# GpSimd's weight sums placed one pass earlier behind row transfers, and ScalarE's copy of a pair placed ahead of the previous pair's activations

## The chip, the cores and the metric

The kernel runs on one core of a Trainium2 chip. Its time is device microseconds for one execution; the times given are medians over several executions. The engines are TensorE (PE; PEld is its weight load), VectorE (DVE), ScalarE (ACT), GpSimd (POOL) and SyncE (SP, which here issues most of the DMAs). Each engine takes its instructions in program order and waits on semaphores for the others.

## The reference

Two stages, all in float32. The first is a linear attention with a decaying state over 4 batches, 8 heads, 768 steps and a head dimension of 48. The second routes each of the 3072 resulting rows of 384 values to one of 8 experts:

```
logits = x @ w_gate                       # 3072 x 8
expert_idx = argmax(logits)               # one expert a token
gate_w = softmax(logits)[expert_idx]
for e in range(8):
    xe = x[expert_idx == e]
    h  = relu(xe @ w1[e])                 # 384 -> 1024
    ye = h @ w2[e]                        # 1024 -> 384
    out[expert_idx == e] = gate_w * ye
```

## The kernel before, in words

The attention takes the first 150 us or so. Tokens are sorted on the way by an indirect DMA into an area of `rows` in HBM for each expert. The experts then run one after another as eight passes (`late`, classes `Pass`, k = 0 to 7) of `WIDTH[k]` tokens; passes 0 and 1 are short, because 160 tokens of theirs have been worked on earlier (`early`). Pass k uses buffers `k % 2` for its weights (`w1s`, `w2s`), tokens and activations, and the passes overlap: while the loop at the end of the program is at pass k, it does the first layer of pass k (`p`) and then the second layer of pass k-1 (`o`).

**First layer** (`quarter(q)`, line 475). From pass 2 on, both layers multiply 2 x 2 blocks with seven products in place of eight, at the price of sums on other engines. The 1024 columns of w1 are taken in four pairs of 128 (in the code a pair is a quarter: `q`). A pair is eleven products into four PSUM banks, pa to pd, and the pairs take two sets of banks in turn (`quads[q % 2]`). PE first computes product `pa` (into the first half of its bank), ScalarE copies it to SBUF (`mida`, line 501), VectorE adds it to the others in five sums (lines 503, 507, 510, 512, 514), and ScalarE applies the ReLU in two activations (lines 511 and 515) that write `hT`. The last product of a pair goes into the second half of bank pa (line 513, traced at line 490 as all products of a pair are).

**Second layer.** `L2` (line 538) takes the tokens over the first 256 (`nt` = 2, `c` = 256) with transposed products and sends blocks of 32 positions to the output by indirect DMAs from GpSimd (`blocks_out`, `scatter`, lines 562 and 669; tile `yo`). `tokens_out` (line 566) takes the first 256 tokens with seven products; it needs four sums of the activations (`inner_sums`, tiles `sums`, VectorE, one behind each pair of the next pass) and four sums of the weights w2, in two halves, so eight instructions of 128 x 384 values a pass (`weight_sums`, line 644, tiles `tums`). Its two results go out as two row transfers (tile `yt`). Pass 1 and pass 0 have `nt` = 1 and no such sums.

**Who works out the weight sums.** In the loop at pass k, GpSimd works out those of pass k-1 at the start, ahead of the first pair of pass k. At the last pass VectorE works out those of pass 6 ahead of everything else there, and GpSimd those of pass 7 behind the row transfers of pass 6. All such sums are traced at line 680 (`op`), the row transfers at line 670.

**The order of the work** is written by hand: the program's order is the order on every engine. On SP the loads stand in the order w1 of pass k+2, w2 of pass k+1, rows of pass k+2 (lines 424, 450, 454). `result` (line 860) spreads the row transfers of the early tokens: a tiny copy on GpSimd waits for one activation (line 862), and one transfer follows.

Of the kernel before, what the change touches and what calls it, by code (L numbers as in the profile page):

```python
# [8 lines left out]
FP32 = mybir.dt.float32  # L9
# [34 lines left out]
def straight(tc, rk, vk, w, w1, w2, out, flag):  # L44
# [173 lines left out]
    def buffers(pool, n, k, x=None):  # L218

        return (x or pool.tile([128, n // 32, Q], FP32, name=f"xs{k}"), pool.tile([128, DT, n], FP32, name=f"xT{k}"),  # L220
                pool.tile([128, FT, n], FP32, name=f"hT{k}"), pool.tile([128, n // 32, 2 * D], FP32, name=f"yq{k}"),
                pool.tile([128, n // 32, 2 * D], FP32, name=f"yo{k}"), pool.tile([128, n // 32], I32, name=f"ix{k}"))

    early_bufs = [buffers(cp, EARLY, f"e{k}") for k in range(2)]
# [207 lines left out]
    class Pass:  # L432
# [3 lines left out]
        def __init__(self, k, s0, n, nt, bufs=None):  # L436
            self.k, self.s0, self.n, self.nt = k, s0, n, nt
            self.c = 128 * nt
            self.e = k
# [35 lines left out]
        def quarter(self, q):  # L475

            n, w, t, sd = self.n // 2, w1s[self.k % 2][q], self.t, quart[q]
            pa, pb, pc, pd = quads[q % 2]  # L480

            def W(m, f):
                return w[:, m, f * 128:(f + 1) * 128]

            def T(m, z):
                return t[:, m, z * n:(z + 1) * n]

            def product(p, at, *ab):
                for j, (a, b) in enumerate(ab):
                    nc.tensor.matmul(p[:, at * n:(at + 1) * n], lhsT=a, rhs=b, start=j == 0, stop=j == len(ab) - 1,  # L490
                                     skip_group_check=True)
# [9 lines left out]
            nc.scalar.copy(a[:, 0:n], pa[:, 0:n])  # L501
            product(pb, 1, (S[1], Y[1]))
            nc.vector.tensor_tensor(u[:, 0:2, 0:n], both(pb), bc(a[:, None, 0:n], [128, 2, n]), op=ALU.add)
            product(pc, 0, (S[0], Y[0]), (W(2, 1), T(2, 1)))
            product(pd, 1, (S[2], Y[2]))
            product(pd, 0, (S[3], T(1, 1)), (S[4], T(2, 1)))
            nc.vector.tensor_tensor(v[:, 0:n], pc[:, 0:n], u[:, 1, 0:n], op=ALU.add)
            f = slice(2 * q, 2 * q + 2)
            second = self.h[:, f, n:2 * n]
            nc.vector.tensor_tensor(second, both(pd), bc(v[:, None, 0:n], [128, 2, n]), op=ALU.add)  # L510
            nc.scalar.activation(second, second, func=ACT.Relu)  # L511
            nc.vector.tensor_tensor(x[:, 0:n], pd[:, n:2 * n], u[:, 1, 0:n], op=ALU.add)
            product(pa, 1, (W(1, 1), Y[3]), (W(2, 1), T(2, 0)))
            nc.vector.tensor_tensor(u[:, 2, 0:n], pa[:, n:2 * n], x[:, 0:n], op=ALU.add)
            nc.scalar.activation(self.h[:, f, 0:n], u[:, 0:3:2, 0:n], func=ACT.Relu)

        def quarter_sums(self, q):

# [47 lines left out]
        def tokens_out(self):  # L566
# [34 lines left out]
                return lambda f: sums[k][:, f, :]  # L601

            def Tm(k):
                return lambda f: tums[k][:, f, :].rearrange("p (m a i) -> p a m i", m=DT, a=2)

            y = self.yt

# [33 lines left out]
            final(1, 0, tr, 0, so[7])  # L641
            scatter(out, it2[:, 1:2], self.yt[1][:, :], N)

        def weight_sums(self, eng=nc.gpsimd):

            if self.nt < 2:
                return
            ws = w2s[self.k % 2]

            for q in range(2):  # L650
                o = slice(2 * q, 2 * q + 2)
                (b11, b12), (b21, b22) = [[halves(ws[q + u])[:, :, z] for z in range(2)] for u in (0, 2)]
                t1, t2, t3, t4 = [x[:, o].rearrange("p f (m c) -> p f m c", m=DT) for x in tums]
                op(t1, b12, b11, ALU.subtract, eng)
                op(t2, b22, t1, ALU.subtract, eng)
                op(t3, b22, b12, ALU.subtract, eng)
                op(t4, b21, t2, ALU.subtract, eng)

        def inner_sums(self, js=range(4)):

# [8 lines left out]
    def scatter(to, at, x, n):  # L669
        s_ = nc.gpsimd.indirect_dma_start(out=to[:, :], out_offset=bass.IndirectOffsetOnAxis(ap=at, axis=0),  # L670
                                          in_=x, in_offset=None, bounds_check=n - 1, oob_is_err=False)
        tc.declare_no_dep(s_.ins, group="sc", reason="each token stands in one row")
        tc.add_to_no_dep_group("sc", s_.ins)

    def halves(x):

# [2 lines left out]
    def op(o, a, b, how, eng=None):  # L679
        (eng or nc.vector).tensor_tensor(o, a, b, op=how)  # L680
# [124 lines left out]
    A_.close()  # L805

    mp = P.enter_context(tc.tile_pool(name="mp", bufs=1))
    bufs = [buffers(mp, CAP, k) for k in range(2)]
    xss = [bufs[0][0], bufs[1][0], mp.tile([128, ng, Q], FP32, name="xs2")]
    nt = 2  # L810
    xgs = [mp.tile([128, nt, 2], FP32, name=f"xg{k}") for k in range(3)]
# [616 lines left out]
```

## Time and profile before

| what | us |
|---|---|
| median of six runs | 383.6 |
| lowest and highest of them | 381.77 and 385.1 |
| the profiled execution | 383.0 |
| its span, from first to last instruction | 381.2 |
| PE busy | 362.5 |
| VectorE busy | 245.7 |
| GpSimd busy | 193.0 |
| ScalarE busy | 140.6 |

In the profile a line of a timeline gives the start, the time taken, the engine, the program line, the operation, the tile written and the tiles read, the shapes, how many instructions were merged, and in brackets how long the engine was idle before and what ended that. "issue" there stands for a wait that no recorded event explains. Tiles stand without their numbers: `X` is one of the banks of the first set of four, `yps`, `dsb` and `tr` make the second. By PE, the loop's round 2 (first layer of pass 2, then second layer of pass 1) runs from 177.5 to 203.5 us, round 3 to 234.6, round 4 to 266, round 5 to 298, round 6 to 329.5; the last round begins with the second layer of pass 6, has pass 7's first layer from 344.6 to 358.4, and its second layer behind it. A matmul on float32 is recorded as two instructions.

### The profile page before, as it was taken

Reading aid. Unit: us, or ns where it says so; the run is one execution under the profiler, and the core shown is the slowest. Engines: PE = TensorE matmul, PEld = TensorE weight load, DVE = VectorE, ACT = ScalarE, POOL = GpSimd, SP = SyncE. Lnnn points to the kernel's source line nnn. Section 1 sums busy time; section 2 is a strip of 40 time slices with the busy share of each in tenths; the row PEclk is TensorE's granted clock in tenths of the full one; section 3 lists DMA queues with packets and bytes.
Section 4 is the critical chain, followed back from the end, with each engine's and each line's share of the span. In section 5 each row is a group of like instructions: output and inputs, shape, how many; then the busy total and the mean of one; then the engine's idle time right before and its main releaser. Section 6 shows DMA issues by size and latency. Waiting matters only on the chain.

```text
span 381.2 us, 9059 instructions
## 1 busy us (share of the span) xinstructions
PE 362.5 (95%) x3371; PEld 335.1 (88%) x3371; DVE 245.7 (64%) x651; ACT 140.6 (37%) x401; POOL 193.0 (51%) x216
## 2 busy tenths in 40 slices
PE   6999999999998999999999999999899999999991
PEld 6788888787887999997998999999799889999890
DVE  8977797697862224055695893796598399665531
ACT  2678787687773310320311212312131131112210
POOL 3379779779853330544117406904922850737241
PEclk9999999999999999999999999999999999999998
DMA  7999797866664783695829528425642833412301
GB/s 205 274 254 244 250 252 230 262 200 204 203 163 168 238 339 75 188 259 172 196 83 249 147 82 223 126 84 176 166 125 89 230 106 104 146 38 93 121 19 48
DMA packets 34981, 65.08 MB, mean 171 GB/s; under 512 B 18378, under 2 KB 19410, under 8 KB 34928
## 3 DMA queue, kind: packets, MB, share of 16 engines
q1 hardware_dynamic: 29392, 49.86, 47.3%
q0 software_dynamic: 3808, 9.84, 7.4%
q10 hardware_dynamic: 1728, 4.72, 3.7%
q8 instruction: 28, 0.46, 0.5%
q14 instruction: 25, 0.20, 0.2%
HBM read 53.29 MB, written 11.26 MB: 169 GB/s over the span
## 4 chain that ended last, share of the span: by engine, by line
PE 88%; issue 5%; DVE 2%; POOL 2%; ACT 1%; DMA 0%; POOLq 0%; DVEq 0%; ACTq 0%
PE X L545 12%; PE X L490 12%; PE X L468 8%; PE X L290 6%; PE tr L591 6%; PE yps L591 6%; PE yps L333 5%; PE yps L490 5%; PE tr L351 4%; PE yps L338 3%; PE tr L578 3%; PE tr L490 2%; PE dsb L490 2%; PE yps L545 2%; PE dsb L591 2%
## 5 line engine op out<-in xcount | busy, mean ns | idle before, releaser
L670 POOL DMA_INDIRECT out_dram<-yo,ix x33 | 32.3, 980 | 92.9 <-DVE ia L572 85.3
L296 ACT ACTIVATE A<-ident,own 128x128 f32<-128x128 f32 x192 | 58.0, 391 | 9.1 <-DVE own L282 8.4
L545 PE MATMUL X<-hT,w2s 128*128 128x96 f32 (+7 forms) x384 | 47.7, 284 | 0.4 <-issue 0.4
L545 PEld LDWEIGHTS X<-hT,w2s 128*128 128x128 f32 x384 | 47.3, 191 | 0.8 <-issue 0.6
L403 POOL DMA_INDIRECT rows<-xb,slot x24 | 30.1, 1253 | 15.3 <-issue 6.7
L511 ACT ACTIVATE hT<-hT 128x416 f32<-128x416 f32 (+5 forms) x23 | 12.3, 536 | 55.0 <-DVE hT L510 53.1
L290 PE MATMUL X<-RK 48*128 48x128 f32 x384 | 30.3, 289 | 1.5 <-DVE RK L259 1.5
L290 PEld LDWEIGHTS X<-RK 48*128 48x128 f32 x384 | 24.0, 187 | 7.2 <-issue 4.3
L259 DVE TENSOR_TENSOR RK<-rk,TT 112x1536 f32<-112x1536 f32 x16 | 27.7, 1733 | 0.0
L265 POOL TENSOR_TENSOR rp<-rk 112x768 f32<-112x768 f32 x15 | 27.3, 1818 | 0.0
L490 PE MATMUL X<-xT,w1s 128*128 128x208 f32 (+5 forms) x120 | 26.0, 331 | 0.0
L302 DVE COPY_PREDICATED A<-strict,X 128x512 f32<-128x512 int32 x32 | 23.1, 738 | 4.5 <-ACT A L296 4.4
L591 PE MATMUL yps<-tums,sums 128*128 128x192 f32 x144 | 25.4, 326 | 0.0
L333 PE MATMUL yps<-A,vk 128*48 128x128 f32 x384 | 24.3, 276 | 0.0
L591 PEld LDWEIGHTS yps<-tums,sums 128*128 128x128 f32 x144 | 23.7, 190 | 0.0
L680 POOL TENSOR_TENSOR tums<-w2s,tums 128x384 f32<-128x384 f32 x20 | 22.2, 1109 | 0.8
L333 PEld LDWEIGHTS yps<-A,vk 128*48 128x48 f32 x384 | 20.2, 123 | 1.9
L490 PEld LDWEIGHTS X<-xT,w1s 128*128 128x128 f32 x120 | 20.9, 190 | 0.5
L736 POOL COPY turn<-own 1x1 f32<-1x1 f32 x14 | 15.0, 1069 | 9.6 <-DVE own L282 9.4
L670 POOL DMA_INDIRECT out_dram<-yt,it x14 | 14.2, 1011 | 10.3 <-DVE yt L616 6.4
L680 DVE TENSOR_TENSOR quart<-w1s 128x128 f32<-128x128 f32 x69 | 19.1, 285 | 0.0
L351 PE MATMUL tr<-sel,yT 112*128 112x104 f32 x128 | 18.3, 285 | 0.6 <-issue 0.6
(205 smaller groups left out, 779.1 us busy)
## 6 DMA issues: line engine op xcount, KB each, us to landing
w1s<-in_w_dram SPq DMA_DIRECT2D x36, 384.0 KB
rk<-in_rk_dram SPq DMA_DIRECT2D x16, 672.0 KB
w2s<-in_w_dram SPq DMA_DIRECT2D x24, 384.0 KB
vk<-in_vk_dram SPq DMA_DIRECT2D x16, 528.0 KB
w2s<-in_w_dram ACTq DMA_DIRECT2D x8, 384.0 KB
xs<-rows SPq DMA_DIRECT2D x16, 169.0 KB
w1s<-in_w_dram ACTq DMA_DIRECT2D x4, 384.0 KB
rows<-zt SPq DMA_DIRECT2D x1, 1248.0 KB
```

The costliest lines, as they stand in the source:

```text
L259: nc.vector.tensor_tensor(RKs[i % 3][0:KP].rearrange("p u (c t) -> p u c t", t=C), x[0:KP].rearrange("p u (c t) -> p u c t", t=C), bc(TT[: ...
L290: nc.tensor.matmul(o, lhsT=r[q, 1, c * C:(c + 1) * C], rhs=r[q, 0, c * C:(c + 1) * C], start=True, stop=True, skip_group_check=True)
L296: nc.scalar.activation(A[:, place(c, h), :], ident, func=ACT.Copy, scale=own[i % 2][:, c, h:h + 1])
L333: nc.tensor.matmul(o(c, h), lhsT=v[:, c, h * D:(h + 1) * D], rhs=A[:, place(c, h), :], start=c < 2, stop=c == 0, skip_group_check=True)
L351: nc.tensor.matmul(trv[c // 4][:, c % 4, :], lhsT=yTs[i % 3][0:KP, c & 1, (c // 2) * C:(c // 2 + 1) * C], rhs=sel[:, c & 1, i % HP, :], st ...
L403: s_ = nc.gpsimd.indirect_dma_start(out=rows[:, :], out_offset=bass.IndirectOffsetOnAxis(ap=slot[b % 2][:, c:c + 1], axis=0), in_=xbs[b % ...
L468: nc.tensor.matmul(p[:, 0:self.n], lhsT=w1s[self.k % 2][f // 2][:, m, f % 2 * 128:(f % 2 + 1) * 128], rhs=self.t[:, m, 0:self.n], start=m ...
L490: nc.tensor.matmul(p[:, at * n:(at + 1) * n], lhsT=a, rhs=b, start=j == 0, stop=j == len(ab) - 1, skip_group_check=True)
L545: nc.tensor.matmul(p[:, 0:n], lhsT=w2s[self.k % 2][f // 2][:, f % 2, m * 128:(m + 1) * 128], rhs=self.h[:, f, self.c:self.n], start=f == 0 ...
L591: nc.tensor.matmul(p[:, at * Z:(at + 1) * Z], lhsT=a(f), rhs=b(f), start=f == 0, stop=f == FT // 2 - 1, skip_group_check=True)
L670: s_ = nc.gpsimd.indirect_dma_start(out=to[:, :], out_offset=bass.IndirectOffsetOnAxis(ap=at, axis=0), in_=x, in_offset=None, bounds_check ...
L680: (eng or nc.vector).tensor_tensor(o, a, b, op=how)
```

## The change

Two edits and what they need.

1. In `quarter`, the two activations of a pair are no longer issued where their inputs are made. They are noted in `self.last` and issued by a new function `relus`, which the next pair calls right behind its own copy (line 501); the loop calls it once more behind the last pair. `result` in pass 2 follows suit: it is called behind pairs 1 and 3 with the same two activations as before.
2. `weight_sums` issues nothing itself. It appends the eight sums of a pass to a list, `aside`; `scatter` issues one of them on GpSimd behind every row transfer, and `rest` issues what is left behind the last. The loop at pass k now does so for pass k itself, around the second layer of pass k-1, so the sums come one pass earlier than they did, and those of pass 6 are on GpSimd too. The tiles `tums` are doubled for it, and the buffers yq, yo and ix of the late passes are cut to the blocks in use, which makes the room.

```diff
@@ buffers
-    bufs = [buffers(mp, CAP, k) for k in range(2)]
+    bufs = [buffers(mp, CAP, k, max(p.g - p.gc for p in late)) for k in range(2)]
-    tums = [mp.tile([128, FT // 2, DM // 2], FP32, name=f"tums{k}") for k in range(4)]
+    tums = [[mp.tile([128, FT // 2, DM // 2], FP32, name=f"tums{j}{k}") for k in range(4)] for j in range(2)]
@@ def quarter(self, q):
             nc.scalar.copy(a[:, 0:n], pa[:, 0:n])
+            self.relus()
             product(pb, 1, (S[1], Y[1]))
...
-            nc.scalar.activation(second, second, func=ACT.Relu)
...
-            nc.scalar.activation(self.h[:, f, 0:n], u[:, 0:3:2, 0:n], func=ACT.Relu)
+            self.last = [(second, second), (self.h[:, f, 0:n], u[:, 0:3:2, 0:n])]
+
+        def relus(self):
+            for o, x in self.last:
+                nc.scalar.activation(o, x, func=ACT.Relu)
+            self.last = []
@@ def weight_sums(self):
-                op(t1, b12, b11, ALU.subtract, eng)
-                op(t2, b22, t1, ALU.subtract, eng)
-                op(t3, b22, b12, ALU.subtract, eng)
-                op(t4, b21, t2, ALU.subtract, eng)
+                aside.extend([(t1, b12, b11), (t2, b22, t1), (t3, b22, b12), (t4, b21, t2)])
@@ def scatter(to, at, x, n):
+        if aside:
+            op(*aside.pop(0), ALU.subtract, nc.gpsimd)
@@ the loop
+    def rest():
+        while aside:
+            op(*aside.pop(0), ALU.subtract, nc.gpsimd)
...
         if k == n - 1:
-            o.weight_sums(nc.vector)
             o.inner_sums()
+            p.weight_sums()
             o.L2()
             o.tokens_out()
-            p.weight_sums()
+            rest()
             for q in range(3):
                 p.quarter(q)
+            p.relus()
...
             else:
-                o.weight_sums()
                 for q in range(4):
...
-                    if k == 2 and q % 2 == 0:
-                        result(p, 2 * q + 1)
+                    if k == 2 and q % 2:
+                        result(p, 2 * q - 1)
+                p.relus()
...
             if k > 0:
+                p.weight_sums()
                 o.L2()
                 o.tokens_out()
+                rest()
                 weights2(o.k + 2)
```

More of the change, by code (lines that the diff above doesn't have):

```diff
@@ L216, in straight, with buffers @@
     ge = EARLY // 32
[L218 to L224, printed above, removed]
+    def buffers(pool, n, k, blocks):
+        return (pool.tile([128, n // 32, Q], FP32, name=f"xs{k}"), pool.tile([128, DT, n], FP32, name=f"xT{k}"),
+                pool.tile([128, FT, n], FP32, name=f"hT{k}"), pool.tile([128, blocks, 2 * D], FP32, name=f"yq{k}"),
+                pool.tile([128, blocks, 2 * D], FP32, name=f"yo{k}"), pool.tile([128, blocks], I32, name=f"ix{k}"))
+    early_bufs = [buffers(cp, EARLY, f"e{k}", ge) for k in range(2)]
     cnt = cp.tile([128, E], FP32, name="cnt")
@@ L438, in __init__ @@
             self.c = 128 * nt
-            self.e = k
+            self.e, self.last = k, []
             self.g, self.gc = -(-n // 32), self.c // 32
@@ L603, in Tm @@
             def Tm(k):
-                return lambda f: tums[k][:, f, :].rearrange("p (m a i) -> p a m i", m=DT, a=2)
+                return lambda f: tums[self.k % 2][k][:, f, :].rearrange("p (m a i) -> p a m i", m=DT, a=2)
             y = self.yt
@@ L642, in tokens_out, with weight_sums @@
             scatter(out, it2[:, 1:2], self.yt[1][:, :], N)
-        def weight_sums(self, eng=nc.gpsimd):
+        def weight_sums(self):
             if self.nt < 2:
@@ L650, in weight_sums @@
             for q in range(2):
-                o = slice(2 * q, 2 * q + 2)
                 (b11, b12), (b21, b22) = [[halves(ws[q + u])[:, :, z] for z in range(2)] for u in (0, 2)]
-                t1, t2, t3, t4 = [x[:, o].rearrange("p f (m c) -> p f m c", m=DT) for x in tums]
-                op(t1, b12, b11, ALU.subtract, eng)
-                op(t2, b22, t1, ALU.subtract, eng)
-                op(t3, b22, b12, ALU.subtract, eng)
-                op(t4, b21, t2, ALU.subtract, eng)
+                t1, t2, t3, t4 = [x[:, 2 * q:2 * q + 2].rearrange("p f (m c) -> p f m c", m=DT) for x in tums[self.k % 2]]
+                aside.extend([(t1, b12, b11), (t2, b22, t1), (t3, b22, b12), (t4, b21, t2)])
         def inner_sums(self, js=range(4)):
@@ L673, in scatter @@
         tc.add_to_no_dep_group("sc", s_.ins)
+        if aside:
+            op(*aside.pop(0), ALU.subtract, nc.gpsimd)
+    aside = []
     def halves(x):
```

## The prediction

> **What bounds the kernel now.** I read the head of the page first, then the chain of work that ended last, then what TensorE waits for, then the timeline of single passes.
>
> ```profile
> span 381.2 us, 9059 instructions
> PE 362.5 (95%) x3371; PEld 335.1 (88%) x3371; DVE 245.7 (64%) x651; ACT 140.6 (37%) x401; POOL 193.0 (51%) x216
> ...
> PE 88%; issue 5%; DVE 2%; POOL 2%; ACT 1%; DMA 0%; POOLq 0%; DVEq 0%; ACTq 0%
> ```
>
> TensorE (PE) is busy for 95% of the span and makes 88% of the chain. The change leaves every matmul as it is, so only PE's idle time can be won. Of the 18.7 us of it, 8.3 us are the tail after the last matmul (the chain leaves PE at 372.9 us, the span ends at 381.2 us), and what lies ahead of 150 us is the attention part; the change touches neither. So I asked for PE's waits from 150 us to the end:
>
> ```profile
> PE yps L490 <- ACT mida L501: 1.9, 2, 1.1
> PE X L490 <- issue: 1.3, 2, 0.9
> PE X L490 <- ACT mida L501: 0.4, 1, 0.4
> PE X L545 <- issue: 0.4, 1, 0.4
> ```
>
> The columns are total, times and longest, in us. These six waits, 4.0 us, are all that the change can reach. More than 4.0 us (1.0%) can't come out of this change; that is the first thing to know of it.
>
> The timeline places them. In pass 5 (its pairs begin at 265.8 us) the wait of the first line looks so:
>
> ```profile
> 272.87 0.53 ACT L511 ACTIVATE hT<-hT 128x396 f32<-128x396 f32 x1 [3.56 <-DVE hT L510]
> ...
> 273.21 0.36 DVE L514 TENSOR_TENSOR midu<-X,midx 128x198 f32<-128x198 f32 x1
> ...
> 273.50 1.05 DVE L680 TENSOR_TENSOR sums<-hT 128x512 f32<-128x512 f32 x1
> 273.61 0.54 ACT L515 ACTIVATE hT<-midu 128x396 f32<-128x396 f32 x1 [0.21 <-DVE midu L514]
> ...
> 274.06 0.30 ACT L501 COPY mida<-yps 128x198 f32<-128x198 f32 x1
> ...
> 274.41 0.30 PEld L490 LDWEIGHTS yps<-toks,w1s 128*128 128x128 f32 x2 [1.40 <-ACT mida L501]
> 274.41 0.60 PE L490 MATMUL yps<-toks,w1s 128*128 128x198 f32 x2 [1.09 <-ACT mida L501]
> ```
>
> The first product of pair 1 was issued at 270.14. ScalarE's copy of it (L501) stands in program order behind both activations of pair 0 (L511, L515), and the second of these waits for VectorE's last sum of pair 0 (L514, 273.21). So the copy runs at 274.06, and the last product of pair 1, which writes the same bank, waits 1.09 us for it. Pass 6 does the same at 306.44, for 0.80 us. Their sum is 1.89 us, the first line.
>
> Lines two and three are another wait, at pair 0 of passes 4, 5 and 6. Pass 4:
>
> ```profile
> 233.14 1.46 PE L591 MATMUL tr<-tums,hT 128*128 128x192 f32 x8
> ...
> 237.73 0.42 DVE L616 SCALAR_TENSOR_TENSOR yt<-tr,xg,so 128x192 f32<-128x192 f32 x1 [3.70 <-PE X L490]
> 237.76 0.33 ACT L501 COPY mida<-X 128x204 f32<-128x204 f32 x1 [3.56 <-PE X L490]
> ...
> 238.14 0.61 PE L490 MATMUL X<-toks,w1s 128*128 128x204 f32 x2 [0.43 <-ACT mida L501]
> ```
>
> The product that L616 reads was done by 234.6, yet VectorE and ScalarE, both idle, start only 3.1 us later. Nothing stands ahead of them: PE's results become visible late. In pass 3 the same copy runs at 204.10, 0.6 us after its product was issued at 203.50. What passes 4 to 6 have at that moment is the load of rows (SP L450, four issues from 232.70) and the row transfers of GpSimd (L670, the yt ones at 235.48 and 238.42) among weight loads. The price is 0.43, 0.41 and 0.92 us, 1.76 us in all.
>
> **Edit 1: the copy of a pair ahead of the activations of the last.** No instruction is added or removed; L511 and L515 of pair q stand behind the copy of pair q+1. In pass 5 the copy then needs only its product (270.14 plus the 0.6 us of pass 3) and runs near 271, while ScalarE is idle until 272.87. The last product of pair 1 starts at 273.32: 1.09 us won, and 0.80 us in pass 6.
>
> What is late next? PE may not write pair q+2's bank before VectorE's L514 of pair q. In pass 5 PE now comes to pair 2 at 273.98, and L514 ended at 273.57. VectorE itself does not get earlier, since the sum at 273.50 stands before its pair 1: L514 of pair 1 still ends at 276.92, and PE comes to pair 3 at 277.66. In pass 6 the same sums give 309.39 against 309.82. So VectorE's slack is 0.4 to 0.7 us, enough, but not much. The delayed activations cost nothing: their readers are a pass later, and the one near reader, the GpSimd copy at 191.14 in pass 2, is moved by a pair in the program too and releases transfers that nothing waits for. **Edit 1: -1.89 us.**
>
> **Edit 2: the sums of the second layer's weights one pass earlier.** Prices:
>
> ```profile
> L680 POOL TENSOR_TENSOR tums<-w2s,tums x20: 994/1002/1485, 206.7 to 354.4; 128x384 f32<-128x384 f32 x20
> ...
> L680 DVE TENSOR_TENSOR sums<-hT x12: 681/686/1546, 208.5 to 360.3; 128x512 f32<-128x512 f32 x12
> ...
> L680 DVE TENSOR_TENSOR tums<-w2s,tums x4: 553/556/559, 330.8 to 333.8; 128x384 f32<-128x384 f32 x4
> ```
>
> (Minimum, median, maximum in ns, then first and last start.) VectorE loses 8 sums of 0.55 us, 4.4 us from 330.1 on. That is off the path: PE runs L545 of pass 6 and the first products there, and needs the activation sums that stand behind only at 338.07, when they have been done for 2.4 us. It wins 0. GpSimd gets these 8 sums: 8.0 us. With the change all 48 stand one behind each row transfer, and those left over behind the last. A transfer is 0.98 us with a gap of 0.30 us, so a pair is 0.98 + 1.00 + 0.30 = 2.28 us instead of 1.29. In the loop's round 4 the first transfer starts at 261.09; the yt transfers, sixth and seventh, which fall beside pass 5's pairs, move from 267.55 and 268.99 to 272.5 and 274.8, and the last sum ends at 277.8, now 278.85. No engine waits for them, as yt and the weight sums have two buffers each, and the sums' reader is a pass away. In the last round it is near: pass 6's sums end at 324.0 + 7 x 2.28 + 1.0 = 341, then six transfers with eight sums take 16 us, to 357. PE reads them at 366.2. The cover is 9 us; if it were gone, each us later would be a us of the end. The weights of pass k were issued for loading a pass before (257.61 for pass 5, wanted at 293), so no sum waits on GpSimd's queue, where the transfers stand behind it.
>
> Where VectorE's two-input sums meet GpSimd's, both stretch: 0.69 to 1.55 us, 1.00 to 1.49. Before pass 7 this is new: four sums at 1.55 us from 329.9 end by 336.1, still before 338.07. The Trainium skill (SBUF — State Buffer, "SBUF: two separate sides") speaks against the change here: VectorE instructions with two SBUF inputs and GpSimd lock each other out of one port for a whole instruction; the rows agree, but by it the meetings only move, and the sum above stays.
>
> What the trace can't show is how late PE's results get with the yt transfers one or two pairs later. Bounds: the delay at pair 0 goes with them and gives back 1.76 us, and with the 0.39 us at 333.6, where the yt transfers of pass 5 also run, 2.15 us; or it stays and comes again in pairs 1 and 2, at 0.41 to 0.92 us in each of three passes, +1.2 to +2.8 us. I take 0, since the row loads stay where the delay begins: in pass 6 the lateness starts before the yt transfer's issue at 299.31. **Edit 2: 0 (-2.15 to +2.8).** The smaller yq, yo and ix buffers and the moved early transfers: 0, as PE has no wait there.
>
> **The sum.** -1.89 + 0. The profiled execution took 383.0 us, 1.8 us of it outside the span, which gives 381.1. It lies 0.6 us under the median of the runs, 383.6; against that it is **381.7 us**, -0.5%. A difference of 0.5%, 1.9 us, is about what a measurement of this kernel can tell from no change, so the forecast lies on the border itself.
>
> **Rivals.**
> 1. *The delay at pair 0 goes too.* For: the yt transfers leave the place where it is seen. Against: the row loads remain. All 4.0 us: 379.6.
> 2. *The wait moves.* The delay meets pairs 1 and 2 and the copy's reader waits there instead. For: 3.0 us of matmuls lie between a pair's first and last product, and the delay was 2.6 to 3.1 us. Against: without bulk loads beside them the delays look shorter (0.7 us at 345.71). +1.2 to +2.8 - 1.89: 383 to 384.5. That the copy gains nothing, as it would if another wait held it, is this time too (383.6).
> 3. *VectorE becomes the bound: slower.* Place: L514 of pairs 1 and 2 in passes 4, 5 and 6. It decides once VectorE is held up by more than its 0.4 to 0.7 us of slack. A delay of 2.6 us then costs some 2 us in each pass: 3 x 2 - 1.9 = +4, 387.7. Against it: the slack in pass 7 was 2 us, so the delayed passes alone are at risk.
>
> **Numbers.** Forecast 0.50, rival 1 0.19, rival 2 0.17, rival 3 0.14. The forecast's own range is 381 to 382.4; half of it is faster by over 0.5%. Faster: 0.26 + 0.19 = 0.45; same: 0.24 + 0.17 = 0.41; slower 0.14. The range leaves out rival 3 and keeps both ends of the unknown delay: 379.5 to 384.5.
>
> **What would show it.** PE's waits on mida at pair 1 gone, and L501 ahead of pair 0's L511 in passes 5 and 6; GpSimd's transfers 2.3 us apart, its last sum by 357; no sum of w2s on VectorE; the copies at pair 0 of passes 4 to 6 still some 2.6 us late. PE waiting on VectorE's L514 would be rival 3; waits on mida in pairs 1 to 3 rival 2. I am wrong if PE's idle time from 190 to 359 us stays near 4 us, or if a sum waits for weights.

## The result, and the profile after

The changed kernel takes **379.16 us** (median of 20 runs, 375.68 to 381.86), the kernel before takes 383.86 us in the same comparison (46 runs). The ratio is **0.9864, with the interval 0.984 to 0.9888**: faster by 1.4%. The prediction was 381.7 us with a range of 379.5 to 384.5, so the kernel is faster than the range allows. What happened is, by its traces, the first rival: the late results at pair 0 are gone too; and it won more than the 4.0 us at which that rival was priced.

The profiled execution took 377.39 us, 375.6 of them in the span (before: 383.0 and 381.2). Line numbers move: the activations of a pair (L511, L515) are now L519, L545 is L550, L591 is L596, L616 is L621, the row transfers are L671, the sums L685. The copy stays at L501 and the products of a pair at L490. The page of the changed kernel, its head and its chain by engine:

```profile
span 375.6 us, 9058 instructions
PE 360.8 (96%) x3371; PEld 335.5 (89%) x3371; DVE 245.9 (65%) x643; ACT 139.9 (37%) x401; POOL 201.5 (54%) x224
...
PE 85%; DVE 5%; ACT 3%; issue 2%; POOL 1%; DMA 0%; POOLq 0%; ACTq 0%; DVEq 0%
```

VectorE has 8 instructions fewer and GpSimd 8 more, as the diff says. "issue", the time in the chain that no recorded event explains, falls from 5% to 2%. The list of PE's waits from 150 us to the end had four lines before; now it has none.

The timeline at pass 4's start, which the prediction showed for the kernel before (there L616 and the copy both ran at 237.7, 3.3 us after the pair's first product at 234.44). Here that product is at 234.94:

```profile
234.95 1.02 POOL L685 TENSOR_TENSOR tums<-w2s,w2s 128x384 f32<-128x384 f32 x1
235.21 0.42 DVE L621 SCALAR_TENSOR_TENSOR yt<-tr,xg,so 128x192 f32<-128x192 f32 x1 [0.69 <-PE tr L596]
235.54 0.33 ACT L501 COPY mida<-X 128x204 f32<-128x204 f32 x1 [0.85 <-PE X L490]
...
240.53 1.26 POOL L671 DMA_INDIRECT out_dram<-yt,it  x1 [0.16 <-issue]
```

L621 and L501 start as soon as their products are done: the copy 0.60 us after the first product was issued. The row transfers of GpSimd stand 2.2 us apart (233.94, 236.14 and 238.33 here), one sum between two of them, and the large ones (yt) begin at 240.53, well inside the pass. In the kernel before they follow each other at 1.29 us:

```profile
234.20 0.98 POOL L670 DMA_INDIRECT out_dram<-yo,ix  x1 [0.30 <-issue]
235.48 0.98 POOL L670 DMA_INDIRECT out_dram<-yt,it  x1 [0.30 <-issue]
```

The four row loads of SP are where they were (L450 from 233.19).

Pass 5, where the copy of pair 1 held the last product for 1.09 us before:

```profile
269.85 0.33 ACT L501 COPY mida<-yps 128x198 f32<-128x198 f32 x1 [3.36 <-PE yps L490]
270.07 0.54 ACT L519 ACTIVATE hT<-hT 128x396 f32<-128x396 f32 x1
...
272.28 0.50 PE L490 MATMUL yps<-toks,w1s 128*128 128x198 f32 x2
```

The copy stands ahead of pair 0's two activations, and the last product (272.28) has no bracket: it waits for nothing.

**Where the time went.** I measure each round by PE, from the first product of a pass's first layer to that of the next. The column "in all" runs from pass 3's first product to the end of the last matmul; I call it the **late part**.

| us | round 3 | round 4 | round 5 | round 6 | second layer of pass 6 | pass 7, first layer | second layer | in all |
|---|---|---|---|---|---|---|---|---|
| before | 30.95 | 31.34 | 32.08 | 31.45 | 15.10 | 13.85 | 14.62 | 169.38 |
| after | 30.95 | 30.64 | 30.04 | 28.98 | 14.46 | 13.84 | 14.62 | 163.53 |

The late part is 5.85 us shorter, though PE's recorded waits were 4.0 us. The start of pass 3 (203.49 before, 203.99 after) is not touched by the change and differs between executions; in the runs below it lies between 199.2 and 208.5. So the late part is the better measure of the change in a single profile, and the ratios are the measure of the time.

### The profile page after: what moved, and what is told of

Read it like the earlier page. It is cut to its first block, busy times and chain, and to the rows that moved or that the text cites. A ratio compares the mean times of both kernels' runs of the same rounds, so it can differ in the third digit from the quotient of the medians.

```text
span 375.6 us, 9058 instructions
## 1 busy us (share of the span) xinstructions
PE 360.8 (96%) x3371; PEld 335.5 (89%) x3371; DVE 245.9 (65%) x643; ACT 139.9 (37%) x401; POOL 201.5 (54%) x224
## 4 chain that ended last, share of the span: by engine, by line
PE 85%; DVE 5%; ACT 3%; issue 2%; POOL 1%; DMA 0%; POOLq 0%; ACTq 0%; DVEq 0%
PE X L550 12%; PE X L490 12%; PE X L468 9%; PE tr L596 6%; PE yps L596 6%; PE X L290 5%; PE yps L490 5%; PE yps L333 4%; PE tr L351 3%; PE tr L490 3%; PE dsb L490 3%; PE tr L583 3%; ACT A L296 2%; PE yps L338 2%; PE yps L550 2%
## 5 line engine op out<-in xcount | busy, mean ns | idle before, releaser
L671 POOL DMA_INDIRECT out_dram<-yo,ix x33 | 33.3, 1009 | 84.5 <-DVE ia L577 79.5
L550 PE MATMUL X<-hT,w2s 128*128 128x96 f32 (+7 forms) x384 | 47.4, 283 | 0.0
L550 PEld LDWEIGHTS X<-hT,w2s 128*128 128x128 f32 x384 | 47.2, 191 | 0.2
L490 PE MATMUL X<-xT,w1s 128*128 128x208 f32 (+5 forms) x120 | 26.0, 331 | 0.0
L596 PE MATMUL yps<-tums,sums 128*128 128x192 f32 x144 | 25.4, 326 | 0.0
L685 POOL TENSOR_TENSOR tums<-w2s,tums 128x384 f32<-128x384 f32 x24 | 24.7, 1028 | 0.4
L596 PEld LDWEIGHTS yps<-tums,sums 128*128 128x128 f32 x144 | 23.7, 190 | 0.0
L490 PEld LDWEIGHTS X<-xT,w1s 128*128 128x128 f32 x120 | 20.9, 190 | 0.5
L351 PEld LDWEIGHTS tr<-sel,yT 112*128 112x128 f32 x128 | 15.6, 191 | 4.5 <-issue 2.0
L685 DVE TENSOR_TENSOR quart<-w1s 128x128 f32<-128x128 f32 x69 | 19.1, 285 | 0.0
L519 ACT ACTIVATE hT<-hT 128x416 f32<-128x416 f32 (+5 forms) x23 | 12.4, 538 | 15.6 <-DVE hT L511 15.6
```

The source lines that it names most:

```text
L351: nc.tensor.matmul(trv[c // 4][:, c % 4, :], lhsT=yTs[i % 3][0:KP, c & 1, (c // 2) * C:(c // 2 + 1) * C], rhs=sel[:, c & 1, i % HP, :], st ...
L550: nc.tensor.matmul(p[:, 0:n], lhsT=w2s[self.k % 2][f // 2][:, f % 2, m * 128:(m + 1) * 128], rhs=self.h[:, f, self.c:self.n], start=f == 0 ...
L596: nc.tensor.matmul(p[:, at * Z:(at + 1) * Z], lhsT=a(f), rhs=b(f), start=f == 0, stop=f == FT // 2 - 1, skip_group_check=True)
```

## The experiments

**Theories.** *The spacing*: edit 2 puts the row transfers 2.2 us apart in place of 1.29, and that removes the late results. A rival, *the copy*: edit 1 does it, as the copy no longer stands behind waiting activations. A rival that was the prediction's own assumption, *the row loads*: SP's loads make the delay. A last rival, *the order*: not the spacing, but that the real sums come one pass earlier and are off the start of the next pass. Each expectation was written before its run; a theory may go by a shorter name there.

The runs fell on five chips, called A to E here; each is compared with the kernel before on its own chip. A number used throughout is the **age of a copy**: from the issue of a pair's first product to the start of L501. A prompt copy at pair 0 has an age of 0.5 to 0.6 us. Before, in the first profile: 3.31, 3.21 and 3.60 at pair 0 of passes 4, 5 and 6.

### Chip A (before: 383.55 us): each edit alone, and the spacing taken away or added

**copy_only**: edit 1 alone, the sums as before.

```diff
-                aside.extend([(t1, b12, b11), (t2, b22, t1), (t3, b22, b12), (t4, b21, t2)])
+                op(t1, b12, b11, ALU.subtract, eng)
+                op(t2, b22, t1, ALU.subtract, eng)
...
-        if aside:
-            op(*aside.pop(0), ALU.subtract, nc.gpsimd)
```

> Edit 1 alone on the kernel before: ScalarE's copy ahead of the previous pair's activations; row transfers 1.29 us apart and the weight sums where they were. Theory S (spacing: PE's results become visible late when row transfers of GpSimd follow each other 1.29 us apart into pair 0; the wait at pair 1 needs this delay and the copy's old place together): waits on mida at pair 1 of passes 5 and 6 gone, those at pair 0 of passes 4 to 6 stay (some 1.8 us recorded); time -2 to -3 us, ratio about 0.993. Rival C (the copy's place is behind all six waits): no PE wait left after 150 us, -5 us, ratio about 0.986.

Measured: 382.98 us, ratio 0.9987 (0.9949 to 1.0025). The late part is 167.49, 1.89 us less than in the first profile of before; that would be a ratio of 0.995, which the interval just holds, so the time does not tell it from nothing. The ages at pair 0 of passes 4, 5 and 6 are 3.22, 3.09 and 2.10: the delay is still there, so it is not the copy's place that removes it. The two largest of PE's waits, of 2.3 us in all:

```profile
PE X L550 <- issue: 0.8, 2, 0.4
PE X L490 <- DVE midu L514: 0.6, 1, 0.6
...
```

The second line is the prediction's third rival, with 0.6 us of it: at 304.81 in pass 6 VectorE's L514, itself behind a late result, holds pair 2. And the copy of pair 1 in pass 6, which no activation stands before, still runs 3.01 us after its product:

```profile
300.81 0.97 POOL L675 DMA_INDIRECT out_dram<-yt,it  x1 [0.30 <-issue]
...
303.31 0.32 ACT L501 COPY mida<-yps 128x190 f32<-128x190 f32 x1 [4.13 <-PE yps L490]
```

ScalarE was idle for 4.13 us beside the second large transfer; the result came late.

**sums_only**: edit 2 alone; the activations stay ahead of the next copy.

```diff
-            self.relus()
...
+            nc.scalar.activation(second, second, func=ACT.Relu)
...
-            self.last = [(second, second), (self.h[:, f, 0:n], u[:, 0:3:2, 0:n])]
+            nc.scalar.activation(self.h[:, f, 0:n], u[:, 0:3:2, 0:n], func=ACT.Relu)
```

> Edit 2 alone on the kernel before: weight sums one pass earlier, one behind each row transfer, so transfers 2.2 us apart; the copy stays behind the previous pair's activations. Theory S: copies at pair 0 prompt (under 0.4 us late), and the waits at pair 1, which were a follow-up of the delay at pair 0, go with it: under 0.6 us of PE waits after 150 us, ratio about 0.987. Rival C: the waits at pair 1 stay at 1.5 us or more, or those at pair 0 stay too; ratio 0.992 to 1.0.

Measured: 375.98 us, ratio 0.982 (0.9756 to 0.9885). The late part is 163.54, that of the whole change; PE has no wait. At pair 0 the ages are 0.60, 0.59 and 0.58. At pairs 1 to 3 the copies still stand behind the activations, with ages of 1.4 to 2.4 us, and that costs nothing: 3.0 us of matmuls lie between the first and the last product of a pair. So in the kernel before, the wait that edit 1 was made for comes from the late pair 0 and the VectorE that is late behind it: the two groups of waits that the prediction added up had one cause. (The same wait can have another: yt_together_b below holds VectorE up by other means.)

**burst**: the whole change, but no sum behind a transfer; all eight come behind the last.

```diff
 def scatter(to, at, x, n):
...
-        if aside:
-            op(*aside.pop(0), ALU.subtract, nc.gpsimd)
```

> The changed kernel with no sum behind a transfer: all eight sums of a pass behind the pass's last transfer, so the transfers are 1.29 us apart again and run into pair 0. Both edits are otherwise in. Theory S: the delay at pair 0 of passes 4 to 6 is back (copies 2 to 3 us late, some 1.8 us of PE waits there), ratio about 0.993. Rival P (it is the sums being a pass earlier and off VectorE, not the spacing, that took the delay away): as the changed kernel, 0.986.

Measured: 386.98 us, ratio 1.0067 (1.0021 to 1.0113). The transfers are 1.29 us apart again, and the delay is back: ages at pair 0 of 3.22 and 2.52 in passes 4 and 5; in pass 6 pair 0 is prompt (0.58) and pair 1 late (3.08). The sums are as early in the program as in the change, and the buffers are cut as there, so neither the order alone nor the smaller buffers remove the delay. The waits (4.7 us in all) hold something that I had not seen:

```profile
PE yps L596 <- POOL tums L683: 3.1, 1, 3.1
PE X L490 <- DVE midu L514: 0.9, 2, 0.6
...
```

In the last round the sums of pass 6 have a reader only some us away: the second layer of pass 6 itself. Here they begin at 331.35, behind the last transfer, and PE stops until 337.80; that stage takes 19.40 us in place of 14.46. In the changed kernel the sixth sum ends at 332.44, and PE, which loads the first of that product's sixteen weights at 332.39, reads it some four matmuls later: about 0.6 us of cover.

**spaced**: the kernel before, with a subtraction of 128 x 384 scratch values on GpSimd behind each row transfer of the late passes.

```diff
 def scatter(to, at, x, n):
...
+        if spaced:
+            op(spaced[0][0], spaced[0][1], spaced[0][2], ALU.subtract, nc.gpsimd)
```

> The kernel before with nothing but spacing: behind each row transfer from round 2 on GpSimd does one subtraction of 128 x 384 values on scratch tiles whose result nobody reads (the buffers yq, yo and ix are cut as in the change to make room). The weight sums, VectorE's eight in the last round and the copy's place stay as before. Theory S: the delay at pair 0 goes and most of the wait at pair 1 with it: under 0.8 us of PE waits after 150 us, ratio about 0.987 to 0.99. Rival P: the waits stay at some 4 us, ratio 1.0, or above it by what the extra 40 subtractions cost.

Measured: 390.11 us, ratio 1.018 (1.0109 to 1.0251); one of its six executions took 2070 us and is not in the ratio. The delay is gone: ages at pair 0 of 0.60, 0.80 and 0.79 (within 0.2 us of prompt), with none of the real sums moved. Pass 4, whose first product is at 233.61:

```profile
232.76 0.99 POOL L670 DMA_INDIRECT out_dram<-yo,ix  x1 [0.17 <-issue]
...
234.21 0.33 ACT L501 COPY mida<-X 128x204 f32<-128x204 f32 x1 [0.85 <-PE X L490]
...
234.95 0.99 POOL L670 DMA_INDIRECT out_dram<-yo,ix  x1 [0.17 <-issue]
```

So the spacing removes it. The expected gain did not come; the time went elsewhere. Ahead of pass 7 VectorE does its eight weight sums beside GpSimd's subtractions:

```profile
329.82 1.47 DVE L684 TENSOR_TENSOR tums<-w2s 128x384 f32<-128x384 f32 x1
329.86 1.01 POOL L684 TENSOR_TENSOR dum<-dum,dum 128x384 f32<-128x384 f32 x1
...
331.39 0.56 DVE L684 TENSOR_TENSOR tums<-w2s,tums 128x384 f32<-128x384 f32 x1
...
341.51 0.93 PE L591 MATMUL yps<-tums,sums 128*128 128x192 f32 x3 [4.82 <-DVE sums L684]
```

The four sums that meet a subtraction take 1.47 to 1.94 us, the four that meet none 0.55 to 0.56; the first activation sum, at 338.67, takes 2.06, and PE waits 4.82 us for the chain. The same eight sums cost PE nothing in the kernel before. The Trainium skill (SBUF — State Buffer, "SBUF: two separate sides") says that a VectorE instruction with two SBUF inputs and a GpSimd instruction that reads SBUF shut each other out for a whole instruction. The trace agrees: each of the four stretched sums ends 0.42 to 0.44 us behind the end of the subtraction beside it (the one at 329.82 at 331.29, the subtraction at 330.87), although by the recorded starts it began 0.04 to 0.48 us ahead of it.

### Chip B (before: 385.37 us): again, with another spacing, and the row loads moved

**after_again** and **sums_again** are the changed kernel and sums_only once more.

> The changed kernel once more, beside the next one on the same chip. Theory N (edit 1 wins nothing once edit 2 is in, since without the delay at pair 0 no copy is late enough to hold PE): from pass 3's first product to the last matmul 163.5 us, as in edit 2 alone, and the two medians within 0.5% of each other. Rival: edit 1 costs or gains 0.5% or more beside edit 2.

> Edit 2 alone once more, beside the changed kernel on the same chip. Theory N: the same time within 0.5%, 163.5 us from pass 3's first product to the last matmul. Rival: a difference of 0.5% or more, as the first runs of the two on different chips had it (0.982 against 0.986 of the kernel before).

Measured: 378.98 us, ratio 0.9827 (0.9775 to 0.988), and 379.44 us, ratio 0.9839 (0.9786 to 0.9893). Both late parts are 163.54. Beside edit 2, edit 1 wins nothing that can be seen.

**gap_long**: the kernel before, with a memset of 128 x 1024 values (0.97 us) on GpSimd behind each transfer of rounds 2 to 6.

```diff
+        if gap:
+            nc.gpsimd.memset(dum, 0.0)
...
+        if k in (2, n - 1):
+            gap[:] = [1] * (k == 2)
```

> The kernel before, with a memset of 128 x 1024 values on a scratch tile (about 1 us on GpSimd, it reads no SBUF) behind each row transfer of rounds 2 to 6, none in the last round; weight sums, VectorE's eight and the copy's place as before, buffers cut as in the change. Theory S (spacing alone ends the delay; what made the earlier spaced kernel slow was that its dummy subtractions read SBUF beside VectorE's two-input sums): copies at pair 0 of passes 4 to 6 within 0.2 us of their 0.6 us, VectorE's sums not stretched by it, ratio 0.985 to 0.992. Rival: a GpSimd instruction behind each transfer costs as such, ratio 1.0 or more.

Measured: 383.58 us, ratio 0.9989 (0.995 to 1.0029): the expected gain did not come. The ages did: 0.60, 0.80 and 0.80 at pair 0 of passes 4 to 6, so a spacing of 2.1 us by work that reads nothing removes the delay too. In the last round, which this kernel leaves unspaced, pairs 1 and 2 have ages of 3.10 and 2.84. What ate the gain are PE's waits of 2.6 us for VectorE (`so`, L609): the eight real sums still run at the start of the next pass, now pushed some 6 us later by the memsets, into VectorE's sums of w1 (`quart`), which take 0.28 us alone and 1.05 to 1.10 at 249.82, 250.94 and 251.91:

```profile
249.27 1.49 POOL L684 TENSOR_TENSOR tums<-w2s 128x384 f32<-128x384 f32 x1
...
249.82 1.08 DVE L684 TENSOR_TENSOR quart<-w1s 128x128 f32<-128x128 f32 x1
```

In the changed kernel the real sums are the spacing, so nothing is pushed.

**rows_late**: the kernel before, with the row loads of passes 4 to 7 moved behind the first pair of the next round.

```diff
+                    if q == 0 and k > 2:
+                        nc.sync.dma_start(mark, p.h[0:1, 1, 0:1])
+                        late[k + 1].load()
...
-        if k + 2 < n:
+        if k < 2:
             late[k + 2].load()
```

> The kernel before with the load of rows for passes 4 to 7 moved behind the first pair of the round (a 4-byte transfer on SP that waits for that pair's activation holds it back); row transfers 1.29 us apart as before. Theory S alone (the burst of row transfers is enough): copies at pair 0 of passes 4 to 6 still 2 us or more late, time as before. Rival R, the one that the prediction took (the row loads make the delay): those copies prompt, the delay at most moved to pair 1 or 2, time -2 to -4 us.

Measured: 387.36 us, ratio 1.0051 (1.0008 to 1.0093). In pass 4, whose first product is at 239.47:

```profile
241.79 0.98 POOL L670 DMA_INDIRECT out_dram<-yt,it  x1 [0.30 <-issue]
...
242.76 0.33 ACT L501 COPY mida<-X 128x204 f32<-128x204 f32 x1 [3.54 <-remote]
...
248.21 0.89 SPq L450 DMA_DIRECT2D xs<-rows  x2
```

The copy starts 3.29 us after its pair's first product with no row load near it; the loads come at 248.21. In pass 5 the age is 2.03. In pass 6 the copy is prompt (0.58), against the expectation, but the results behind it are late: VectorE's first sum of pair 0 (L503) starts 4.14 us after the pair's first product, 1.56 in the changed kernel, and the loads are issued only at 311.49, 4.9 us later. So the delay needs no row loads, and with that falls the reason for which the prediction took 0 for edit 2.

### Chips C, D and E (before: 373.21, 372.9, 373.06 us): no delay to remove

I went on to ask how much spacing is needed and behind which transfers. These runs were to answer it: **by_twos** (two sums behind every second transfer), **yt_together** (no sum behind the two large transfers, so that those stay 1.3 to 1.6 us apart), **yo_together** (the small transfers stay together, four sums behind each large one) and **gap_short** (gap_long with 128 x 256 values, 0.33 us, a spacing of 1.47 us). The first three are edit 2 alone with another rule in `scatter`:

```diff
+        sent.append(to)
+        if len(sent) % 2 == 0:
+            for _ in aside[:2]:
+                op(*aside.pop(0), ALU.subtract, nc.gpsimd)
```

for by_twos, and for yt_together and yo_together

```diff
+        if aside and to is out4:
+            op(*aside.pop(0), ALU.subtract, nc.gpsimd)
```

```diff
+        if to is out:
+            for _ in aside[:4]:
+                op(*aside.pop(0), ALU.subtract, nc.gpsimd)
```

> Edit 2 alone, but the sums two at a time behind every second row transfer: transfers come in twos 1.29 us apart, the twos some 4.4 us from start to start. Theory M (what counts is how many transfers are under way, so the mean pitch): copies of pa prompt as in edit 2 alone (0.6 us at pair 0, at most 2.1 us at pairs 1 to 3, where they stand behind activations), 163.5 to 164.5 us from pass 3's first product to the last matmul. Rival D (two direct neighbours are enough): copies 2 to 3 us late in pair 0 or 1 of passes 4 to 6, 167 to 169 us.

> Edit 2 alone, with no sum behind the two large row transfers (yt, 128 rows of 1536 bytes), so these two are 1.29 us apart and the five small ones (yo, 384 bytes) 2.2 us; the left-over sums follow. Theory Y (the two large ones together make the delay): copies at pair 1 or 2 of passes 4 to 6, where the yt transfers now run, over 2.5 us. Theory M: all prompt.

> Edit 2 alone, with no sum behind the small row transfers and four behind each large one: five small ones and the first large one 1.29 us apart, the second large one some 4 us on. Theory Y: copies at pair 0 prompt, under 1 us. Theory M: copies at pair 0 of passes 4 to 6 late by 2 us or more, as with all transfers back to back. In the last round the sums come too late for pass 6's second layer in either case, which costs PE some 3 us.

> The kernel before with a memset of 128 x 256 values (about 0.27 us) behind each row transfer of rounds 2 to 6: a pitch of some 1.45 us in place of 1.29 and 2.1. Theory M: the copies at pair 0 of passes 4 to 6 are late by some part of the 2.6 to 3.0 us of before, 1 to 2.5 us. Rival: any instruction between two transfers ends the delay, under 0.3 us late.

Measured on chip C, where the kernel before takes 373.21 us and not 383:

| | ratio | interval | late part |
|---|---|---|---|
| by_twos | 1.0015 | 0.9971 to 1.006 | 163.54 |
| yt_together | 1.0161 | 1.0053 to 1.0269 | 169.58 |
| yo_together | 1.0048 | 1.0006 to 1.009 | 165.51 |
| gap_short | 0.9998 | 0.9964 to 1.0031 | 163.54 |

None is faster. Before reading anything into that I needed the kernel before itself in a profile on such a chip: **before_here**, on chip D, unchanged, with three of the others again.

> The kernel before itself, with a profile of its own beside the next three on the same chip. Theory H (the delay depends on the chip: on the chip of the last four runs the kernel before took 373.2 us, on the two earlier ones 383.6 and 385.4): where its time is near 383 us or above, copies at pair 0 of passes 4 to 6 are 2 us or more late and the part from pass 3's first product to the last matmul takes 169 us; where it is near 373 us, all copies of pa are prompt and that part takes some 163.5 us. Rival: the time differs only ahead of pass 3, and the copies are late on every chip.

> Edit 2 alone with two sums behind every second transfer, again, beside the kernel before on this chip. Theory M (the mean pitch counts): prompt copies and 163.5 to 164.5 us from pass 3 on, also where the kernel before shows the delay. Rival D (two direct neighbours are enough): late copies in pairs 0 to 3 of passes 4 to 6 there.

> The kernel before with a memset of some 0.27 us behind each row transfer of rounds 2 to 6, again, beside the kernel before on this chip. Theory M: where the kernel before shows the delay, part of it is left: copies at pair 0 of passes 4 to 6 are 1 to 2.5 us late. Rival: none left, under 0.3 us.

> Edit 2 alone without a sum behind the two large row transfers, again, beside the kernel before on this chip. In its first run its copies at pairs 2 and 3 of passes 5 and 6 came 2.5 to 4.5 us after their product. Theory Y (two large transfers 1.29 us apart beside the weight loads make the delay, on any chip): the same again, 167 us or more from pass 3 on. Rival X (one disturbed execution): prompt copies, 164 to 165 us.

before_here: 372.64 us, ratio 0.999 (0.9948 to 1.0032), late part **163.53**: to 0.01 us that of the changed kernel. PE has no wait. Pass 4, whose first product is at 230.67:

```profile
228.92 1.91 SPq L450 DMA_DIRECT2D xs<-rows  x4
...
230.41 0.98 POOL L670 DMA_INDIRECT out_dram<-yo,ix  x1 [0.30 <-issue]
...
231.27 0.33 ACT L501 COPY mida<-X 128x204 f32<-128x204 f32 x1 [0.85 <-PE X L490]
...
231.70 0.98 POOL L670 DMA_INDIRECT out_dram<-yt,it  x1 [0.30 <-DMA w2s<-in_w_dram]
```

The same transfers, 1.29 us apart, beside the same row loads, and the copy is prompt (0.60 us). The delay depends on the chip, or on the time of the run: each chip was used in one stretch only, and C, D and E came after A and B, so the two can't be told apart here. by_twos_b had 1.0019 (0.9985 to 1.0053), gap_short_b 1.0021 (0.9985 to 1.0056), yt_together_b 1.0158 (1.0112 to 1.0205). by_twos and gap_short therefore say nothing of the spacing that is needed: there was no delay to remove.

yt_together and yo_together are slower for reasons of their own. In yo_together the sums of pass 6 come too late for the near reader (PE waits 1.7 us for them). In yt_together_b three sums are left over and run in a row:

```profile
271.04 1.02 POOL L680 TENSOR_TENSOR tums<-w2s,tums 128x384 f32<-128x384 f32 x1
...
271.16 3.37 DVE L680 TENSOR_TENSOR sums<-sums,hT 128x512 f32<-128x512 f32 x1
...
272.98 1.00 POOL L680 TENSOR_TENSOR tums<-w2s,tums 128x384 f32<-128x384 f32 x1
...
277.66 0.60 PE L490 MATMUL yps<-toks,w1s 128*128 128x198 f32 x2 [1.51 <-ACT mida L501]
```

VectorE's sum, 0.69 us alone, ends at 274.53, 0.55 us behind the last of the three (passes 4 and 6 have the same, 3.31 and 3.42 us); VectorE's five sums of the pair, then the activations, then the copy behind them are late by that much, and PE waits 1.51 us. So the time that its expectation gave to large transfers close together (167 us or more) came about, but not by late results of PE: the copies of pair 0 are prompt (0.58 to 0.60). Here a copy ahead of the activations should help, but I did not try it.

Last, on chip E, the whole change where there is no delay (**after_c**), and **gap_short_c**:

> The changed kernel once more. Theory H (what the change removes is a delay that only some chips have): where the kernel before takes 381 us or more on this chip, ratio 0.980 to 0.989; where it takes some 373 us, ratio 0.997 to 1.003, with 163.5 us from pass 3's first product to the last matmul in both. Rival: a gain of over 0.5% also where the kernel before takes 373 us.

> The kernel before with a memset of some 0.27 us behind each row transfer, once more. On a chip with the delay, theory M: part of it is left, the copies at pair 0 of passes 4 to 6 come 1 to 2.5 us late; rival: none left, under 0.3 us. On a chip without it: as the kernel before, and nothing is learned of the gap.

after_c: 373.07 us, ratio **1.0001** (0.9975 to 1.0027), late part 163.53. gap_short_c: 375.11 us, ratio 1.0018 (0.9985 to 1.005), late part 163.53. On such a chip the change wins nothing and costs nothing. It brings a chip of the first kind to the late part of the second; the stretch ahead of pass 3, which it leaves alone, keeps its difference (it ends at 199.2 to 201.9 us on chips C, D and E, and at 202.4 to 208.5 on A and B).

## Why the prediction was wrong, point by point

- **"I take 0, since the row loads stay where the delay begins"** (edit 2) is the step that failed. rows_late has the delay without the loads; sums_only, spaced and gap_long lose it with the loads in place; copy_only and burst keep it with the transfers 1.29 us apart. On a chip that has the delay it is there when the transfers are 1.29 us apart and gone when they are 2.1 to 2.3 us apart. The outcome was in the prediction's bounds (-2.15) and was rival 1, to which it gave 0.19. The argument against the row transfers (the lateness of pass 6 begins before the yt transfer's issue) looked at the large transfers alone; the five small ones ahead of them, 1.29 us apart too, were not weighed. In the prediction's sum it is the term of edit 2: 0 was put in, and all that the change won came by it (sums_only alone has the whole gain of the late part).
- **"More than 4.0 us can't come out of this change"** failed too: 5.85 us came out. The idle time in the list is not all that a wait costs. The prediction's own lines show it: at 274.41 PE is idle for 1.09 us, its weight load for 1.40, and load and matmul start together, where otherwise the load runs beside the matmul ahead. That is 0.3 us more for each wait, 4.0 + 6 x 0.3 = 5.8. (Set beside the changed kernel matmul by matmul, each of the six costs 0.25 to 0.27 us more than is listed, and a pause at 310.2, too short for the list, 0.2 us.) The same sum in the other kernels (listed waits + 0.3 us each, against late part less 163.53):

| | listed waits | their number | sum | measured |
|---|---|---|---|---|
| before | 4.0 | 6 | 5.8 | 5.85 |
| copy_only | 2.3 | 6 | 4.1 | 3.96 |
| rows_late | 3.9 | 6 | 5.7 | 5.53 |
| gap_long | 3.3 | 5 | 4.8 | 4.90 |
| yt_together_b | 4.7 | 4 | 5.9 | 6.05 |
| yo_together | 1.7 | 1 | 2.0 | 1.98 |
| burst | 4.7 | 5 | 6.2 | 7.69 |
| spaced | 8.3 | 6 | 10.1 | 12.07 |

It fits but for burst and spaced, and there the rest is in one product. In burst, behind the wait for the weight sums, twelve matmuls take 3.78 us, where all sixteen take 2.76 in the changed kernel: most of them start 0.32 us apart in place of 0.16. In spaced the same product does so behind its wait of 4.82 us, which makes 1.7 of the 2.0 us. Why is open; yo_together has the same product wait 1.7 us without it.
- **Edit 1, -1.89 us.** The mechanism and the order of instructions are as predicted, and alone it shortens the late part by 1.89 us in one profile of each kernel. That this is the predicted figure is partly chance: the waits left are others than predicted (0.6 us for L514, two of 0.4 at L550). Beside edit 2 it is worth 0, since without the late pair 0 its wait does not arise. The prediction's sum of two independent terms was wrong in form.
- **Rival 3**, VectorE's slack of 0.4 to 0.7 us: its mechanism shows in copy_only and burst, at 0.6 and 0.9 us, not at the 6 us it was priced at; with both edits it does not arise.
- **Edit 2's own costs, 0**: right in the result. The transfers are 2.2 us apart (predicted 2.28), no sum waits for weights, and the eight sums taken off VectorE win nothing (before_here, which has them there, has the same late part). But the cover was misread. "PE reads them at 366.2" is the reader of pass 7's sums; those of pass 6 are read in the same round, with about 0.6 us to spare and not 9. (By the prediction's own numbers they would have ended at 341, behind that reader, which stands at 338.07 in the kernel before.) burst and yo_together show the price where it is missed: 3.1 and 1.7 us.
- **The time.** Against the profiled execution of before, 383.0 - 5.85 = 377.2; the profiled execution after took 377.39.

What stays open: why some chips have the delay and others not, and by what the row transfers hold back PE's results; how small a spacing ends it, and whether the small or the large transfers need it. The runs made for that fell on chips without the delay (D by the profile of before, C and E by its time). Whether the recording of a profile has a part in the delay is open too: the ratios agree with the profiles (5.85 us of 383.9 is 1.5%, the measured gains on chips with the delay are 1.4 to 1.8%), but every execution on record comes with its span and its granted clock, so none of them is known to have run unrecorded.

The traces hold two more marks. What comes late is PE's own semaphore update (the signal that an instruction is done), not the reader: in the first profile of before, updates of PE come at 237.64, 237.68 and 237.75, 0.04 and 0.07 us apart; in the changed kernel no two of them from pass 3 on are closer than 0.22 us. Such bunches stand in before, copy_only, burst, rows_late and the last round of gap_long, and in none of after, sums_only, spaced and before_here. And in every profile of the first comparison and of chips A and B many updates have no record, with the delay or without: PE's are 363 to 370 for 387 instructions that make one, those of DMAs 2676 to 3035; on C, D and E they are 387 to 389 and 3721 to 3750. This mark goes with the chips or the time, not with the kernel, and it is not settled what it means.

## What to carry to other kernels

When a consumer starts microseconds after its producer was done, with nothing ahead of it on its engine, look for bursts of DMA issues on GpSimd beside it, and put work that is due anyway between them; filling the gaps with idle work cost as much as it won (gap_long) or more (spaced). In a kernel like this one, take the listed idle time of a bound TensorE as a lower bound of what a wait costs, and ask whether two waits have one cause before their gains are added. Repeat a gain of one or two per cent on several chips and at several times: this one is 1.4 to 1.8% on the first and nothing on the later ones.

## What the runs showed of the hardware that was not expected

- The kernel before takes 383.6 to 385.4 us on some chips and 372.9 to 373.2 us on others. Of the 9.9 us between the spans of its two profiles (381.2 and 371.3), 5.85 lie in the late part and 3.8 ahead of pass 3; the 3.8 were not studied.
- PE's results became visible to idle engines up to 3 us late (ages of 2.0 to 3.6 us in place of 0.6) while GpSimd issued row transfers 1.29 us apart, and not at 2.1 to 2.3 us, and only on some chips or at some times.
- A transfer that follows another takes GpSimd 0.98 us and 0.30 us of gap; behind a sum or a memset the gap is 0.17 us.
- Three GpSimd sums in a row held a VectorE sum of two SBUF inputs for 3.37 us in place of 0.69: VectorE did not get its turn between them. One subtraction alone stretched a sum of 0.56 us to between 1.47 and 1.94. The rule quoted under spaced speaks of one whole instruction; the three in a row go beyond it. It is not always so: in gap_long, from 249.27, four short sums of VectorE and four of GpSimd's took turns, 1.05 to 1.10 us each in place of 0.28.
